# Diagonal attention scores as products on 32x32 tiles of the TensorE array, with another stored order

## The chip, the cores and the metric

The kernel runs on one core of a Trainium2 chip. A core has a matrix engine (TensorE, "PE" in the profile; its weight loads are listed apart as "PEld"), a vector engine (VectorE, "DVE"), a scalar engine (ScalarE, "ACT"), GpSimd ("POOL") and a queue that issues transfers (SyncE, "SP"). The metric is the device time in microseconds of one execution, as the median of several runs; lower is better.

## The reference

Two independent layers on 2048 tokens of width 640, joined side by side in the output. Layer A is a short causal filter of k, multiplied by v, then a long convolution over the whole sequence (by Fourier transforms), times q. Layer B is attention with 32 heads of 20 channels in four segments of 512 tokens: causal softmax within a segment, and a linear memory of the segments before. Only layer B is touched:

```python
qs, ks, vs = (q[:, :, s].copy(), k[:, :, s].copy(), v[:, :, s].copy())
logits = jnp.einsum('bhqd,bhkd->bhqk', qs, ks) * scale + mask
p = _softmax(logits, axis=-1)
a_dot = jnp.einsum('bhqk,bhkd->bhqd', p, vs)
...
num = jnp.einsum('bhld,bhde->bhle', pq, M)
den = jnp.einsum('bhld,bhd->bhl', pq, z)[..., None] + 1e-06
a_mem = num / den
o = g * a_mem + (1.0 - g) * a_dot
M = M + jnp.einsum('bhld,bhle->bhde', pk, vs)
```

Here `mask` is strongly negative where the key lies behind the query in time, so of the 512 x 512 scores of a segment and head only the lower triangle counts.

## The kernel before, in words

**Units.** Layer B is worked in eight units `u`: segment `u // 2`, half `u % 2` of the heads (16 heads, as four groups `gg` of four heads `hl`). Layer A is worked in five channel blocks `dp` and mixed in between. The transposed keys and queries of a unit lie in the tile `KQT`: the 32 partitions from `32 * hl` on belong to head `hl` of each group, 20 of them channels, one the bound that keeps the exponentials small, the rest mask rows.

**Fills.** The scores of a head group are made in "fills" of 512 columns and four heads: two groups of two PSUM banks, one bank a head. `fill` records the products on PE and then two exponentials on ACT, each over two banks, that write the tile `ET`. There are three kinds: "A" (`below`: blocks under the diagonal), "J" (`joined`: blocks of two head groups in one fill) and "D" (`diagonal`: the four 128 x 128 blocks on the diagonal). With five fills for two head groups a unit has ten, of them four of kind D: 32 D fills in the kernel. `weighted` then multiplies `ET` with the values `Va` and with the memory `Mbd`, in products of shape 128x128; DVE divides (`rr`, `o`, `o_s`).

**The diagonal fill.** `diagonal` records 32 products. First sixteen of keys with queries: for each of four key blocks `kc`, one for each head, 32 rows of the array (the head's partitions) and all 128 columns (the block's keys), 128 queries moving. Their 32 rows include the mask rows, which blank the coarse parts of a block's upper triangle. Then sixteen mask products on 32x32 tiles of the array: for each sub-block `i` of 32 keys and each head, `mleft` times `mright` (both in the constant `pack`) adds a large negative number to the fine triangle of all four blocks at once. All accumulate in the head's bank. In the profile the score products are `ps<-KQT 32*128 32x128` and the masks `ps<-pack 32*32 32x128`; the products of A and J fills are `ps<-KQT 21*128`.

**Order.** Nothing schedules at run time. `Recorder` collects 1446 operations (a whole fill's products are one operation, its two exponentials two more), and `issue` writes them out in the order of the table `ORDER`, with PSUM banks from the table `BASE`. Each engine works through its own instructions strictly in that order, and waits are set from the data. The string `EVICT` says for each of 235 evictions of PSUM whether ACT (0) or DVE (1) copies it. Almost all profile rows carry the line of `issue`, L259, so they are told apart by tile names.

Of the kernel before, what the change touches and what calls it, by code (L numbers as in the profile page):

```python
# [924 lines left out]
ORDER = r"""
c-jrs17i>h7zNOKKjd1rYuUE#mTlX%Z7$ccZQHhOoA3RJb5bBFaw8DQkP@j73#pL?X^|Z1kRBNj8}X44aRFpR9^^$NWI{m{LSaNiR768&WJOG5K{n(=6a*kL5+fcGAU_<5qzH;44iZar6hI6KlwwFN;U$8^lr)l6
nxHM3qa})?1WKY5N~1MWNI8^88H7SaDT{0pNwOmsk|4X}kY>m!L=f6QPzAXpx8#vT$cemC9W_uJiVCQRv{Du6#84A;P#3jO5A6^Gl~5Tu&=jpu4bdc)M3>l-M3PDiWR~{GBK6S_jgUYZBcY^}RFY3ZBaXzC4(N{F
=z%M;1Yyt_U65Z2NLVyLM--Ay=!stFgTCmBg3=G&kW2<3xeP=I;z@kzk3krWAsCJ*5>)~uvSgG@(q9Hh1*s@Kq>?N|ddVOoq_7N=a3~^6(Njjsa2X?|q>QY<N|csi7%Ssss*FH!DItq6PzK3RDJkP+f=rg8GDV8X
NGwBTS&ks-CB3DeOp{eujnP<)HCT(XQbo$kC>bpirJPKX=`spK0scfysVeKR9@S(Qs>^OPlEzX?#-O&;ks2}%d(cGc%3jQnda?l<F&5)7Q(8+K*@o@-DZgYB-b!29ft?7C37C#P@=p57X8gu1nJx9Dp-?Acumnp3
*@CT@BmXc&R86O#g|w8pGEYQX$tU?OpXHD2!&FShBpk$RIfOS7R=>zsX)4X7nJkn=au(+hMuRb5PT~}%;UX5uejGqJ4XtwkjiA499_{1;!s{jckWSKBx=2@PFCC<#tdkA0UQXi-E~A@tmxy{8e=!$VFb_v@469|0  # L930
1ZZTPftfgt6NsX-FdJ*-DwfJJc`qO2CYH-L`7ZlpzckewXr@s$n*ISPJRr_cTp=rEm4xPXgyCQLCyOOSmdHnmp$qU0%K6wR(bZU$5l~%g=vLV#*ARm-xm)(i9@#EO5R026HaE)_xs8|_OJnOnIV6YW7Iw%^*(I*u
aR;?|7x!@wp)?BHXdI2owt8Hu@ubw#`r1XKF)Z8Z35m`JsHsOJuEx`Fe1u3Ep2y?|PRVIGDi3i+&Ppwfz;kk5F33f>B#&`f+UpZ^)~D#I&GjW-poJ#Y<eE%tYX|M9b+myt)JED^BQg>bX-iG4tu%m<`5f^zfezJS
`V6n|8t?EParg<Jkwg<}Dow3vGy%J5T5Y1~^bJ~Tdd;A3kx>IRK2vBWO{pL75s4X(NmxXSYIjY}K*nVc&8)>V9aAwi(=#cPF^l%nteQ=;YYL`h4z12K?4-RlE%)nd&8cs+k7i&lt*aSXTnA_g?W_IthThbY`b3}V
Rr!kknu#@8Pzz~c9jJr!n%<OKa$WE0J<Y;|%*sT(Bbk|vHF#HYYhHb(&oz(M;%9xU@ASSt&>YOC`SrTokVb64!TJT+*^u>EpVy>-e$qOu%ON^kM`$T6t!1>V_SDDvQD5muZOkuPPRr|8y(jmjqE^yxT0uLoBfo29
9i?M5NUP{*En`2ms^(-T{?c38nYs8t%32fN*2y|mr)XshvYJ-QUPx}{VN<@8-#S*uX+^7K<25fUv#33j=W<7j*&qF@6LgYJ)Z4O_%?QiKYFgcDSaVL(={iGa>MUKXA-Y8W>1=Jm{0!nlc_feJiO|Ga@`tX_Rk~8w
u>ga0j?UG2I$sy)LT$y?tim>I%cZ(p3)?a+#P?dnN?AL8(Dq!X>$S9PW<f5}!Ysmvx<R{eqi)hix>>jARxQRC`tpAyR_hwwrbStn#aV*oxK>|@*?PLwvrx8OtJn_Rsa;v$x-+zewOzVf_h>h6Vh`@s;#R_{S{N&5
<*k8j<X{fraE@R}>(2p<XpyXu)wVhoU;{abLph8+S(2sL&>GuFj$$|qZyUIayIGzU*wi9eWQ%G$xRX(ApT@LU*34pC9P7<KjBC*>hHYVA_G5FaYw_%<w6N$_&3bVwTiP~mX9a6*X)K+svcq=7#<G=_W*Mfmw3gbM
SR0FPZEZAD*?CKE87+fduxobR#&HZ2*mx$iM3&f+SW>%am+XKhw-gp=$MuAsveTByGFuj#$QyQmH|>ZX)q`wjl~|Dzc+lEgSL<foZ50pMaht?@mdx(j2|H<r^spY{VV=}e+R3`uWZt)|md&zT4(n_=?V%;}T=vKU
J-MgwBRtC9*4O&jRl8+Vc#Ow6m5*&2^H^TXXZfvw-L@Xq({kHEEohm&mmSkIe$LW*7N5a8_Q0OlQ_JJe?V08Ee%9YQSVx=A1)R?Tmd?}rOdhpkc7i84$tK$rdtoo_l@+qAp3P_T6i;)Y4YFArY(s3Q&E-^^X1P4K
ujXZ&Zu2<I_HZxH*cCf#Gi;^}w|xxee$KKv9AP7El#REER>()&7#nL7EQCur&I<ZsF5wxzw)ghIF6(K%q95%7&vOk6`x(8cmvpuj@JxPIQ+rOIYx8WrEwF`lmccg1u5*#y;C<faWft`-{A71{mk;=mpRJgGvBh?d  # L940
S9y((c$2qS-0$(KUg8o9v8A@mmfH$@WAE&(t+ds4PD}WCU1KHv34hox%itOPF&A<Xf7)03Zr?1WFJme%?O{Bem+~@R)|WG^m-FBD$DZ-8J?BOKGdTSzBl-Vb_zDKNxqB!N?JIdfBYSw?ViA3-Met3w*`jzfkM1!%
rbqRce8E^A+v9j#kLTt66)SrckMBXA&ue&1ujQ|q-`{Ypt+#cy!8TfU&*5)b!7KVZ7V!jL$rE}aPwZ8_x+n2!{(;+Vhb8r)Ufb(<UEgEFe5Y-*_x#Bp+-o1X&vscWZ|$GB-#)XR@3#8hz#DoaZ{v-<gLm|=?Bq?n
sefTJZ|*Jp8@qW+@8RA3J5@|vLdkF+;lKEsf7#aC`vD6rfB27KB%Fkm&fd;P`Y4A`M0$EJ@9llOt9SAKKG_HOKp*6Ny`K;EAwJs2_&lHPGkl7V^>IGmXM3>E@tHo?r}{LX<x70AFYxg`!6*78U+5ve$o~UpIlx>
"""
# [76 lines left out]
```

## Time and profile before

| | us |
|---|---|
| median of three runs (270.0 to 271.64) | 270.61 |
| the profiled execution, its own time | 267.98 |
| its span, first to last instruction | 266.2 |
| busy: PE / DVE / ACT | 257.2 / 245.0 / 242.8 |
| PE, score products of D fills (512) | 13.7 |
| PE, mask products of D fills (512) | 8.8 |
| ACT, exponentials (160) | 158.5 |

How to read it: each engine's busy time is the time in which at least one of its instructions was under way. A product on PE is shown from its start until its result has landed, so products overlap one another; the distance between starts says how fast they follow, not their length. A group row gives line, engine, operation, output and inputs, the shape on the array as rows*columns, the moving data, the count, the busy time and the mean length in nanoseconds. In a table of stretches the columns are the stretch and its length, the busy time of each engine with its instructions, the granted clock of TensorE as a share of full speed, the share of the DMA engines and GB/s.

### The profile page before, as it was taken

The page shows a single profiled execution, that of the slowest core. Times are in us where ns is not written, and L with a number is a line of the kernel's source. Part 1 is how long each engine was busy: PE and PEld are TensorE (multiplying, and loading weights), DVE is VectorE, ACT ScalarE, POOL GpSimd, SP SyncE. Part 2 cuts the span into 40 slices and gives each one's busy share as a digit, 9 for nine tenths or more (in the row PEclk, how much of TensorE's full clock was granted, in tenths as well). Part 3 has the DMA queues.
Part 4 walks back from the last instruction along what each step waited for, and adds up shares of the span by engine and source line. Part 5 has one row for each costly group of instructions (what it writes and reads, how often), then busy time and mean ns, then how long its engine had stood idle before and what let it go on. Part 6 is the DMA issues. An engine that isn't in the chain of part 4 may idle for free.

```text
span 266.2 us, 10257 instructions
## 1 busy us (share of the span) xinstructions
PE 257.2 (97%) x4471; PEld 192.8 (72%) x4471; DVE 245.0 (92%) x406; ACT 242.8 (91%) x361; POOL 2.6 (1%) x9
## 2 busy tenths in 40 slices
PE   8999999999999999999999999999999999799994
PEld 3787777768777868768777778777777777556882
DVE  2679799999999999999999999999999999989951
ACT  2478999999999999999999999999999999989943
POOL 3000000000000000000000000000000000000000
PEclk9999999999999999999999999999999999989999
DMA  6999699969979799998999999776937379226142
GB/s 176 245 286 204 153 214 196 250 180 158 164 160 234 153 226 142 161 231 199 110 248 189 220 192 194 101 164 143 170 89 184 81 133 137 55 64 147 38 98 99
DMA packets 127945, 43.86 MB, mean 165 GB/s; under 512 B 118455, under 2 KB 125516, under 8 KB 127772
## 3 DMA queue, kind: packets, MB, share of 16 engines
q1 hardware_dynamic: 127772, 43.14, 82.1%
q8 instruction: 35, 0.57, 0.9%
q0 software_dynamic: 128, 0.07, 0.2%
q14 instruction: 10, 0.08, 0.1%
...
## 4 chain that ended last, share of the span: by engine, by line
PE 82%; DVE 10%; ACT 4%; issue 3%; DVEq 0%; ACTq 0%
PE ps L259 82%; ACT ET L259 3%; DVE F L259 2%; DVE pq L259 2%; DVE Kh L259 1%; DVE Xh L259 1%; DVE o_s L259 1%; DVE o L259 1%; DVE vt L259 0%; DVE KQ L259 0%; DVE rr L259 0%; DVE qabs L259 0%; DVE Y L259 0%; ACT outb L259 0%; DVE outb L259 0%
## 5 line engine op out<-in xcount | busy, mean ns | idle before, releaser
L259 ACT ACTIVATE ET<-ps 128x1024 bf16<-128x1024 f32 x160 | 158.5, 1057 | 3.3 <-PE ps L259 2.7
L259 PE MATMUL ps<-wqkv,xT 128*128 128x320 bf16 x480 | 77.2, 301 | 0.3 <-ACT ET L259 0.3
L259 PEld LDWEIGHTS <-xT 128*128 128x128 bf16 x640 | 58.3, 98 | 26.0 <-issue 4.7
L259 PE MATMUL ps<-Va,ET 128*128 128x21 bf16 x1280 | 41.0, 172 | 0.0
L259 PEld LDWEIGHTS <-ET 128*128 128x128 bf16 x1280 | 38.7, 96 | 2.1 <-issue 1.2
L259 PE MATMUL ps<-KQT 32*128 32x128 bf16 (+3 forms) x896 | 33.4, 242 | 1.0 <-ACT ET L259 0.7
L259 PEld LDWEIGHTS <-Wf 128*128 128x128 bf16 x320 | 29.7, 98 | 6.4 <-issue 1.7
L259 PE MATMUL ps<-wo,xT 128*128 128x320 bf16 (+4 forms) x160 | 25.7, 304 | 0.4 <-ACT ET L259 0.4
L259 ACT CAST KQ<-ps 128x320 bf16<-128x320 f32 x54 | 24.2, 487 | 1.5 <-PE ps L259 1.3
L259 PEld LDWEIGHTS <-KQT 32*128 32x128 bf16 (+1 forms) x896 | 14.1, 92 | 15.5 <-issue 13.6
L259 PE MATMUL ps<-vt,Wf 128*128 128x256 bf16 x160 | 22.9, 273 | 0.0
L259 PE MATMUL ps<-kT,Wf 128*128 128x256 bf16 x160 | 21.1, 273 | 0.2 <-DVE pq L259 0.2
L259 ACT ACTIVATE F<-ps 128x512 bf16<-128x512 f32 x33 | 20.0, 633 | 1.3 <-PE ps L259 0.8
L259 ACT CAST F<-ps 128x512 bf16<-128x512 f32 x34 | 20.0, 635 | 0.8 <-PE ps L259 0.4
L259 PE MATMUL ps<-Y,Wi 128*128 128x256 bf16 x160 | 20.3, 273 | 0.1
L259 PE MATMUL ps<-Mbd,PqT 128*128 128x84 bf16 x96 | 18.0, 202 | 1.1 <-ACT ET L259 0.9
L259 DVE TENSOR_TENSOR Y<-Y,pq 128x2048 bf16<-128x2048 bf16 (+1 forms) x20 | 18.7, 946 | 0.0
L259 DVE TENSOR_TENSOR pq<-Xh,Kh 128x2048 bf16<-128x2048 bf16 x15 | 18.3, 1217 | 0.0
L259 PEld LDWEIGHTS <-Wi 128*128 128x128 bf16 x160 | 15.1, 98 | 2.6 <-issue 0.4
L259 ACT ACTIVATE PP<-KQ 128x1280 bf16<-128x1280 bf16 x12 | 15.8, 1314 | 1.2 <-DVE KQ L259 1.2
L259 PEld LDWEIGHTS <-kr 128*128 128x128 bf16 x116 | 14.4, 148 | 1.9 <-issue 0.6
L259 DVE TENSOR_TENSOR pq<-ps,pq 128x512 bf16<-128x512 f32 x20 | 13.6, 683 | 0.2 <-PE ps L259 0.2
...
## 6 DMA issues: line engine op xcount, KB each, us to landing
...
```

The source lines that it names most:

```text
L259: f(*[fix(a) for a in args], **{k: fix(v) for k, v in kw.items()})
```

## The change

`diagonal` no longer uses `block` with 32 rows. Each score product of 32 rows and 128 columns is split by keys into four on 32x32 tiles of the array: sub-block `i` of 32 keys goes to the columns and PSUM partitions from `32 * i` on. Four rounds (one a key block) of sixteen products follow each other, then the sixteen masks as before: 80 products in a fill instead of 32, all on 32x32 tiles. The values in PSUM are the same. `block` loses its argument `rows`. The tables `EVICT`, `ORDER` and `BASE` are replaced.

```diff
-        def block(bank, hl, g, kc, q0, n, rows=DH + 1, **kw):
-            r = slice(32 * hl, 32 * hl + rows)
+        def block(bank, hl, g, kc, q0, n, **kw):
+            r = slice(32 * hl, 32 * hl + DH + 1)
             nc.tensor.matmul(bank, lhsT=KT[r, g, 128 * kc:128 * kc + 128], rhs=QT[r, g, q0:q0 + n], skip_group_check=True, **kw)
...
         def diagonal(gg):
             def parts(heads):
                 for kc in range(4):
-                    for hl, bank, r, g in heads:
-                        block(bank[:, 128 * kc:128 * kc + 128], hl, gg, kc, 128 * kc, 128, rows=32, start=(kc == 0), stop=False, grp=g)
+                    for i in range(4):
+                        for hl, bank, r, g in heads:
+                            nc.tensor.matmul(bank[32 * i:32 * i + 32, 128 * kc:128 * kc + 128], lhsT=KT[r, gg, 128 * kc + 32 * i:128 * kc + 32 * i + 32],
+                                             rhs=QT[r, gg, 128 * kc:128 * kc + 128], start=(kc == 0), stop=False, grp=g, skip_group_check=True)
                 for i in range(4):
                     for hl, bank, r, g in heads:
...
-EVICT = ("0001000000001001000010010000000001000100000000000100000000000000000010100010010001001000010010000100001001000000000000100"
+EVICT = ("0001110000101000001000010000000100100000000000000000010000000000000001100011000000000110010000000010000010000000000000"
...
 ORDER = r"""
-c-jrs17i>h7zNOKKjd1rYuUE#mTlX%Z7$ccZQHhOoA3RJb5bBFaw8DQkP@j73#pL?X^|Z1kRBNj8}X44aRFpR9^^$NWI{m{LSaNiR768&WJOG5K{n(=6a*kL5+fcGAU_<5qzH;44iZar6hI6KlwwFN;U$8^lr)l6
+c-jq?gO(To3<NjHrnYU{wyi7fYU^s-wr$(CZQHiZf0#EjDG&pZ5djgA65){#u@DcjkqD`f7^#s4X^{><eiT4VBu6r&M*<W?ArwXiWJX40LJ`D=qbQ0Y3$h{`k{}17AS!YrI<g}v5^5sNgS<$saS>f(XdEQh6dG0=
...
```

Three places show what that does to the streams.

The first is PE at the first D fill of the program (unit 0, head group 0), where each product has its weight load ahead of it; `KQT0_96` is the tile `KQT` of the first half, and the last two numbers of a row are the output's partitions and columns. Before:

```order
L259 MATMUL ps_61<-wqkv_79,xT0_105 128x320
L259 LDWEIGHTS KQT0_96 [waits DMAHW5_49]
L259 MATMUL ps_61<-KQT0_96 128x128 [waits Activation_49]
L259 LDWEIGHTS KQT0_96
L259 MATMUL ps_61<-KQT0_96 128x128
...
L259 LDWEIGHTS pack_85 [waits DMASW2_49]
L259 MATMUL ps_61<-pack_85 32x4x32
```

And now:

```order
L259 MATMUL ps_61<-wqkv_79,xT0_105 128x320
L259 LDWEIGHTS KQT0_96 [waits DMAHW6_49]
L259 MATMUL ps_61<-KQT0_96 32x128 [waits Activation_49]
L259 LDWEIGHTS KQT0_96
L259 MATMUL ps_61<-KQT0_96 32x128
...
L259 LDWEIGHTS pack_85 [waits DMASW0_49]
L259 MATMUL ps_61<-pack_85 32x4x32
```

Between the first score product and the first mask there were 16 pairs of load and product that write 128 partitions; now there are 64 that write 32. The masks write 32 partitions in both, so the shape no longer changes inside the fill. The first product's wait, for ACT to have emptied its banks, stays at the head of the fill.

The second is ACT in the stage in which the last units' scores are worked (tiles `ET_...` are exponentials, `Va` and `bT` evictions). Before:

```order
L259 ACTIVATE ET_123<-ps 128x1024 [waits PE_49]
L259 ACTIVATE ET_123<-ps 128x1024 [waits DVE_49]
L259 ACTIVATE ET_120<-ps 128x1024 [waits PE_49]
L259 CAST Va_95<-ps 128x16x20 [waits DVE_49,PE_49]
L259 ACTIVATE ET_120<-ps 128x1024
L259 ACTIVATE ET_119<-ps 128x1024 [waits PE_49]
L259 ACTIVATE ET_119<-ps 128x1024
L259 ACTIVATE ET_121<-ps 128x1024 [waits PE_49]
L259 CAST bT_117<-ps 128x128 [waits DMAHW1_49,PE_49]
L259 ACTIVATE ET_121<-ps 128x1024 [waits DVE_49]
```

And now:

```order
L259 ACTIVATE ET_123<-ps 128x1024 [waits DVE_49,PE_49]
L259 ACTIVATE ET_123<-ps 128x1024 [waits PE_49]
L259 ACTIVATE ET_120<-ps 128x1024 [waits PE_49]
L259 ACTIVATE ET_120<-ps 128x1024 [waits DVE_49]
L259 ACTIVATE ET_119<-ps 128x1024 [waits PE_49] x2
L259 ACTIVATE ET_121<-ps 128x1024 [waits PE_49]
L259 ACTIVATE ET_121<-ps 128x1024 [waits DVE_49,PE_49]
```

The fills follow in the same order; one eviction of values has moved to a later place on ACT, and that of the bounds (`bT`) to DVE.

The third is DVE at the end of the program (`pq` is layer A's output, `xT` the transposed attention output of the last segment, `PP` its projection). Before:

```order
L259 TENSOR_TENSOR pq0_87<-ps_61,pq0_87 128x4x128 x3
L259 CAST xT1_106<-ps_61 128x512
L259 TENSOR_TENSOR pq0_87<-ps_61,pq0_87 128x4x128
L259 RECIPROCAL rr0_126<-ps_61 128x32
L259 TENSOR_TENSOR o_s0_118<-ps_61,rr0_126 128x8x80
L259 RECIPROCAL rr1_127<-ps_61 128x32
L259 TENSOR_TENSOR o_s0_118<-ps_61,rr1_127 128x8x80
L259 CAST PP_89<-ps_61 128x512 x2
```

And now:

```order
L259 TENSOR_TENSOR pq0_87<-ps_61,pq0_87 128x4x128 x4
L259 RECIPROCAL rr0_126<-ps_61 128x32
L259 TENSOR_TENSOR o_s0_118<-ps_61,rr0_126 128x8x80
L259 RECIPROCAL rr1_127<-ps_61 128x32
L259 TENSOR_TENSOR o_s0_118<-ps_61,rr1_127 128x8x80
L259 CAST xT1_106<-ps_61 128x512
L259 CAST PP_89<-ps_61 128x512 x2
```

The one eviction of `xT` has moved behind the last divisions: DVE takes another of the five pieces than before, and ACT the one that was DVE's.

More of the change, by code (lines that the diff above doesn't have):

```diff
@@ L919 @@
 TAP2 = (2, 3, 4)
-EVICT = ("0001000000001001000010010000000001000100000000000100000000000000000010100010010001000010010000100001001000000000000100"
-         "000000000010100100000100000000000000001101001010100000000001001000110001101010101110100101000000100000000100010001001")
+EVICT = ("0001110000101000001000010000000100100000000000000000010000000000000001100011000000000110010000000010000010000000000000"
+         "001100000001001101000000000000010000001101001000000000100101010001000100110101001000100000000110100000110010000110100")
 KQW, FW, WW = 1, 1, 1
@@ L925 @@
 ORDER = r"""
-c-jrs17i>h7zNOKKjd1rYuUE#mTlX%Z7$ccZQHhOoA3RJb5bBFaw8DQkP@j73#pL?X^|Z1kRBNj8}X44aRFpR9^^$NWI{m{LSaNiR768&WJOG5K{n(=6a*kL5+fcGAU_<5qzH;44iZar6hI6KlwwFN;U$8^lr)l6
-nxHM3qa})?1WKY5N~1MWNI8^88H7SaDT{0pNwOmsk|4X}kY>m!L=f6QPzAXpx8#vT$cemC9W_uJiVCQRv{Du6#84A;P#3jO5A6^Gl~5Tu&=jpu4bdc)M3>l-M3PDiWR~{GBK6S_jgUYZBcY^}RFY3ZBaXzC4(N{F
-=z%M;1Yyt_U65Z2NLVyLM--Ay=!stFgTCmBg3=G&kW2<3xeP=I;z@kzk3krWAsCJ*5>)~uvSgG@(q9Hh1*s@Kq>?N|ddVOoq_7N=a3~^6(Njjsa2X?|q>QY<N|csi7%Ssss*FH!DItq6PzK3RDJkP+f=rg8GDV8X
@@ L929 @@
[L929 to L940, printed above, removed]
@@ L941 @@
-S9y((c$2qS-0$(KUg8o9v8A@mmfH$@WAE&(t+ds4PD}WCU1KHv34hox%itOPF&A<Xf7)03Zr?1WFJme%?O{Bem+~@R)|WG^m-FBD$DZ-8J?BOKGdTSzBl-Vb_zDKNxqB!N?JIdfBYSw?ViA3-Met3w*`jzfkM1!%
-rbqRce8E^A+v9j#kLTt66)SrckMBXA&ue&1ujQ|q-`{Ypt+#cy!8TfU&*5)b!7KVZ7V!jL$rE}aPwZ8_x+n2!{(;+Vhb8r)Ufb(<UEgEFe5Y-*_x#Bp+-o1X&vscWZ|$GB-#)XR@3#8hz#DoaZ{v-<gLm|=?Bq?n
-sefTJZ|*Jp8@qW+@8RA3J5@|vLdkF+;lKEsf7#aC`vD6rfB27KB%Fkm&fd;P`Y4A`M0$EJ@9llOt9SAKKG_HOKp*6Ny`K;EAwJs2_&lHPGkl7V^>IGmXM3>E@tHo?r}{LX<x70AFYxg`!6*78U+5ve$o~UpIlx>
+c-jq?gO(To3<NjHrnYU{wyi7fYU^s-wr$(CZQHiZf0#EjDG&pZ5djgA65){#u@DcjkqD`f7^#s4X^{><eiT4VBu6r&M*<W?ArwXiWJX40LJ`D=qbQ0Y3$h{`k{}17AS!YrI<g}v5^5sNgS<$saS>f(XdEQh6dG0=
@@ new lines @@
+AsSjCjfT@~npK;kI7*=eN<)!d%OMiVqdCf;I%=RKYC=!}RZtc=G^f@=F67dj$gO!a00~hM1|krR5rk%_jTWebs;GuaXo(OAuMsq{CefH$8Fdj^^J){M)z*lm!DxsENU7;Gs&+s$&8%6pBf6j~>Z2Y)q7B-j2jXi_
+q|#34jBe<K-bkSB&>e9#pXS#B+8%un8r?OD_Rx453SG4?7NMJF)QFl%BWZsO)*+fylj&tGq)X68`(XeEqJmb^ike<C=wKAo#VD*pupBE8Tl;DpEv2hbTGwDG%IHcI*OFR9SD}P1#WD=TaLh+P?XM#+2t#$4R@N#S
+2BUPe_ST{rpvAPTmeVmhNyln=9f@(;K*wuCZKR{I6T47Vt7)JHX-%!JHMEx2);c;-Cu>U$*4@~H&kC8MZ*&1#=~k@8Hmt)S{i0KKBR1i!{=hV?tJ_gu>*;VEp(Aw%He)@;V1jPJES;{S5EdISKnH41?WM2uwa(C)
+I$P)HIE=+!jK@SY(@AKq6L1jw&_WO37e4BKeA0#Zp+EJPPQh;#Qwwd4wTU)Wvon~hwD}s!PN2QE);4+p7jY6laTYVtK_{cF&O$pqj8h0}rxC_F>Lpyp0u5)K^c>FPgLc*~8s7e5p03sPIu+BfPLJRyBHC=s!B>3O
@@ new lines @@
+Rk~Uu*)bePWSfo|SffjHnO?(EeW&mBH~t`sMKzZYvRC)%SN*0}A+lc&L8Y<5n%Hu^f)%<_O(-E{p)S@x`d1g}7Tv1bw7S)>P;vv;5nW<PNQ-XK>=t(E9^I`m>>Fa*c8w{qWP@(hd6<h$x>;{xhknNaJ*aLW?2y*6
+x^^3Z7Gyg$w1kmkdR&`YGmBs+G_pjIIM&+QSXc=scW@7f^{C#(eZ;kgh$_(}mL1Wm5)Ren0fMcS)wB9`QcvkwJ+0v-f}GRy+QA;-3C`#Ry{MNowk5G-med;9D>Srf5>eXPW3;nKQqyW#LhERWthu$Y#1_w<;|1bd
+Cwq!#7-WO(EfQE9NoA?+CEg*nw6sRH&#vf4d_thS#v8<wG}gtETMA2QX)T?lw+xm{GFm2kj}Pc<MXadBmqe0W(n%^wFU72@C6+9f)v{T3OCfP3rDTwdl3K3mb<JU!t-Ga>w30-UN_)#`J*>Euv{zQb5=c$yX}#>V
+C6pj}Y)|Zt-L>9U&<a^?>uY^1i+o05>u3G#jb)O|a@}s&UCk!<w42qC0hZhH*j2k`Uy#?X>TSKF_w2r9l^pWXZs<VEWpC}K){(lB&+^+Rt0hmZfYp=Q^1+7KFdJ&m?2CQ22J*<(NPTH2rL44-v9k8n%2|0EZrNp|
@@ new lines @@
+wUu^K!A4jkX)G13l2x`U7RUgrYVD<ie6tBQ(SkV1nn+W*Y1Qn$-m)K7ojK*F73C<a!P{1hqiu|pVOi#qihO79?U&_|-}cffF}IAh@wQI>{1@j_9cRz9GOKW*J=eTaS^nB&n_^QfzpRzT_ClxGbemy|?3O;zhuTb<
+%W}&nEC1uIoMp3Zg|(0ZGRMB#OsgU#WUd)oO0cw&dA7us*?fDXk9Da9NNZ^$g`^Y<N>M2+#bmvZ5A2~8kp;Ha*4sKO%;NIgUf2fPXq#-at&}2MW!1Prw%ArH%{5km&Jf%r8)dbXm5>ZzXog}(DJONg-FDbc+htv4
+w^d~wmScH_X9RAunykf$EGc`eI9IX+UuqZGYeS?YYqON}kua>sq0(78$p9HB-K4x!kiODS!f}`klI}8C8Za#T%W#Rrow7@!Fa~2X7GpCq>$8XSlsJsb&9X)ITU174LpI`8*(TB1OL|LVZkHXBhUs{KY1xDaIYLTH
+8EML^tSHy`L{l;qM@vgyU?sW8W^B%QY{4;di0PS{!ED9W%)pF1V23$UMoD}oU_vHhVkY4^o@X+q;5a$SQ#@wLdECazb>84zX5w+4uoKM8gLcTWaKDU~19H;tunjvgDerNDbmn0@V#nBp$vuTX;6cgCY|PF>(w;e(
@@ new lines @@
+leyTDN&T=qWCyO2BhrJ(yeIQ8FDFSaPLzDi&jNhJ+&n7B<R))%vUFv4cH<Eq<yq$O+sx}%n8u&6Ak%tpKIRm8!l}}SnLUg5Wm`UFJC5fBPLo2M$gG~tr^|6UA@|vj{W*XGIf#=uh0pndlQ~09$|<?T!Mx1VJj30x
+M^;NZPw%s32&Zy7XUR;N#$0~N_DXKwCv#*dhjBPZa3s&lTq)?II8VlK9LMq{7s^pvEQ{o{6!KSm#|w7J-t)9Ak<q+pA2@?K{j!~tD^}Rg%Nd)^Ih@ORoX-VZ$eEnQGjdOE$$hykm*ld1<YyN33-XEA<bhn5D{@ut
+$XzMsi@2CexRlGdoGW-k9?EOpl*e+`&e<Dg@|0fO-|{<u@{y$S`LaO1@CU!LgfEqn{*9qLw1@H3UcgIxDPJZ}rHq&LU;NEK{L5z&!6Q0+6<1UIe=MBt9?8RcIA0-8B!pj-kiL=OeG?;lRFC4DxrJ-^LZW#LkM8CC
+yshPOc`h+MmdExuUfwHv6))m(J;3964G;8u{!(5^kZ1QCp20JEeqYD+tl*XWjl7n(Qqkjk0#E3PJh3P7s$Siz`8#<pySbHnSkr5JE#J$1{2)Vo19xyIhx#_Q@Rq)vA0^o9cwMjO^}T_&_4eM#ze{6p;!XXBwDV8W
@@ L944 @@
+&_7FO{~}#{kPr4|-rT>*Px<<P6sWt{)kCQ3e*Tg_@>_=aaBt<UJ*0-x&>BYn%Kt>GY8&t1oqURS^lskWdw5Up<ukmu_wl~o&-?oTAK?>xj1TltKH5k6SfA+=eX39L$v(}e`#7KF<9)U-^aZ}i=lEQo=ktBB{{!DY
+z+3
 """
 BASE = r"""
-c-mD`2@=F049aEv|Bp8U+S%!NGzyXsGc&iEIp!<d_$ynp?uoV~;xUmuBPV{wIX$-uIGde;#lW}cYv2uQ&dSI^??E`w2KEGp<Cg19m!1N5LZ3t5#`)nmqj9sKi1-9+K}AAA;T~1CvPmG%Ta7mwBcREECR@A=68nR0
-+&K6a`<+Ae;GBy3UyWG7qi7)qhXz)iDi~q*p;$>(Nm0WM)`G0p$Bo=l2<BHW+xm+&ILX$~=TdicE%3HHUC)*4OT)vI?obz%YR$iXwKVy3JLvXG=&UvB?a7;RC!~16{f3UME@EE<=B0XWFnxIvUwZF5yE++N>TQ2+
@@ L948 @@
-wyMe(`{^Q%u7+xTc|(<JC~|dH+7B1i1#$
+c-mD`36caM2t&^Q|9By!9k;9610ji#5SJs`e@aR8%0zlTJ!(g?_uk{=Oho(4aqhi0?5gL<n~eERM+%6B3PpVZcQ_0P%OgN4;tNh3*bdYn!=MS63>p+?f~bRU^gDh7moht%71Y1Hj$MK$p<&m8dk>FZu61F3aPWTB
+KZJ=md=li&sH{Hl$&h2L3*xVub=aw3GZi>~)hSgg84Pz-VC?OJtAdt&Ke-tB=u@gYa3`V8_!a^c>v|&3>E&Xc>v>-E^)|>DSP2-Cud2Ljupf+L(Z9tq-de79<^Q_8ks|UzEZ9ZG7uM^?B7AjDMM*dPS$!TIcAm2H
+6zFl^N&j_^Kl7(qh-U23MH!|)$U6n9
 """
```

## The prediction

> **What bounds the kernel now.** First the page: its span, its engines, and the chain of waits by engine.
>
> ```profile
> span 266.2 us, 10257 instructions
> PE 257.2 (97%) x4471; PEld 192.8 (72%) x4471; DVE 245.0 (92%) x406; ACT 242.8 (91%) x361; POOL 2.6 (1%) x9
> ...
> PE 82%; DVE 10%; ACT 4%; issue 3%; DVEq 0%; ACTq 0%
> ```
>
> PE is on the chain for 82% of the span, but DVE and ACT are busy for over 90% too. A mean over stages says little, so next comes the table of busy time by stretch (us busy of each engine, then the granted clock).
>
> ```profile
> 0.00:27.00 27.00, 25.06 (x213) 18.59 (x214) 18.78 (x49) 15.97 (x31) 2.65 (x9) 1.00 0.98 230
> 27.00:215.00 188.00, 187.71 (x3360) 141.87 (x3359) 185.21 (x297) 185.78 (x279) 0.00 (x0) 1.00 0.92 175
> 215.00:246.00 31.00, 28.35 (x599) 19.72 (x596) 29.53 (x43) 29.83 (x39) 0.00 (x0) 0.94 0.51 99
> 246.00:263.00 17.00, 16.12 (x308) 12.60 (x307) 11.50 (x20) 11.16 (x15) 0.00 (x0) 1.00 0.24 64
> ```
>
> In the long middle stretch PE idles for 188.00 - 187.71 = 0.3 us, ACT for 2.2 and DVE for 2.8: all three are full, and PE is only the fullest. From 215 to 246 us PE idles 2.65 us, and the other two less. The chain in order of time says the same:
>
> ```profile
> 26.36 55.11 PE ps L259 x887
> ...
> 81.48 19.91 PE ps L259 x366
> ...
> 107.52 34.75 PE ps L259 x596
> ...
> 142.28 72.33 PE ps L259 x1345
> ...
> 229.34 2.90 ACT ET L259 x3
> ...
> 246.34 16.14 PE ps L259 x306
> ```
>
> PE sets the pace from 26 to 214 us and from 246 to 262 us; between them the chain jumps among DVE, ACT and PE, as in the row of the exponentials (ACT ET) at 229.34.
>
> **The change part by part: the fills.** The edit touches 32 diagonal fills (eight units, four head groups). This is one of them in the timeline of PE and of its weight loads (start, length, shape, count):
>
> ```profile
> 39.81 0.39 PE L259 MATMUL ps<-skd,kr 128*128 128x256 bf16 x3
> 40.14 0.40 PE L259 MATMUL ps<-KQT 32*128 32x128 bf16 x16
> 40.47 0.28 PE L259 MATMUL ps<-pack 32*32 32x128 bf16 x16
> 40.68 0.31 PE L259 MATMUL ps<-wqkv,xT 128*128 128x320 bf16 x1
> ...
> 40.14 0.23 PEld L259 LDWEIGHTS <-KQT 32*128 32x128 bf16 x16
> 40.47 0.14 PEld L259 LDWEIGHTS <-pack 32*32 32x32 bf16 x16
> ```
>
> ```profile
> L259 PE MATMUL ps<-KQT 32*128 32x128 bf16 x512 | 13.7, 217 | 1.0 <-ACT ET L259 0.7
> ...
> L259 PE MATMUL ps<-pack 32*32 32x128 bf16 x512 | 8.8, 226 | 0.0
> ```
>
> The sixteen score products (each 217 ns by the group row) run as four rounds of four. Their last one starts 0.40 - 0.217 = 0.18 us after the first, so a round takes 0.18 / 3 = 0.06 us. The masks do not start 0.06 us after the last round but at 40.47, which is 0.47 - 0.32 = 0.15 us after it: changing the shape from 32x128 to 32x32 costs 0.15 - 0.06 = 0.09 us. The sixteen masks start within 0.28 - 0.226 = 0.054 us, 3.6 ns apart. The next product of full shape starts 0.16 us after the last mask. The fill, from its first product to the next work, takes 40.68 - 40.14 = 0.54 us.
>
> After the change there are 64 score pairs (a weight load and a product each), in four rounds of sixteen. A round is bounded by the stream, 0.06 us, and by sixteen pairs at 3.6 ns, 0.058 us; I take 0.06. Four rounds make 0.24 us, then the masks follow in the same shape: 0.054 us to the last one, 0.16 us to the next work, 0.45 to 0.46 us in all. That saves 0.085 us a fill, 32 x 0.085 = 2.7 us. Upper bound: pairs at 3.6 ns without any step, 80 x 0.0036 + 0.16 = 0.45 us, saves 0.09. Lower bound: weights are not ready when a round starts. A small load's record lasts 0.14 - 15 x 0.0036 = 0.09 us, which would make rounds of 0.15 us and a fill of 0.81 us, 0.27 us longer than now. The nearest row on this is a product that is tiled by columns and loads new weights on each tile for four rounds:
>
> ```profile
> 195.91 0.40 PE L259 MATMUL ps<-qabs,A 128*16 128x128 bf16 x16
> ...
> L259 PE MATMUL ps<-qabs,A 128*16 128x128 bf16 x112 | 2.8, 220 | 0.2 <-DVE A L259 0.2
> ```
>
> Its rounds are (0.40 - 0.22) / 3 = 0.06 us apart, so loading lay beneath the stream there, and I take the loads as hidden.
>
> The Trainium skill speaks against this: "TensorEngine Tiling (Array Packing)", section "Gotcha 2: Feature Incompatibilities", says that column tiling excludes the fast weight load, and "TensorE: Matmul & The Clock Gate", section "LDWEIGHTS (loading the stationary operand)", prices a load at its columns over 1.2, an estimate of 27 ns for 32 columns. Four such loads in the open would make 0.11 us and eat the saving; the trace's 0.06 us rounds on column tiles do not show one in the open, though with 16 columns only.
>
> **The other edits.** Counted in the two stored orders, the changes of shape outside the fills go from 170 to 173: 3 x 0.09 = +0.3 us on PE. Evictions change engine: DVE gets two more and ACT two fewer (51 instead of 49 of 235). The two rows of a typical one cost nearly the same:
>
> ```profile
> L259 ACT CAST KQ<-ps 128x320 bf16<-128x320 f32 x54 | 24.2, 487 | 1.5 <-PE ps L259 1.3
> ...
> L259 DVE CAST KQ<-ps 128x320 bf16<-128x320 f32 x10 | 4.9, 497 | 1.3 <-PE ps L259 1.3
> ```
>
> So DVE gains 1.0 us and ACT loses 1.0 us of work over the run; from zero to all of that falls into the middle stretch, and I take half. It lies beneath PE as long as DVE has idle time there. The stored order moves operations by a few places, in the end stage too, where the last evictions swap engines one for one; I count that at zero, with 0.5 us to either side for its transfers (SP issues the same 157, some earlier and some later). The added instructions must be fetched:
>
> ```profile
> q8 instruction: 35, 0.57, 0.9%
> ```
>
> PE's rows in the stored program go from 8944 to 12016, a third more; by this row that is a third of 0.9% of the DMA engines' span, which I put at zero.
>
> **What reaches the end.** The fills by stretch, with the masks' group (sixteen a fill):
>
> ```profile
> 27.00:215.00 188.00, 6.90 (x400) 3.45 (x400) 5.22 (x15) 0.00 (x0) 1.00 0.92 175
> 215.00:246.00 31.00, 1.38 (x80) 0.69 (x80) 0.19 (x1) 0.00 (x0) 0.94 0.51 99
> 246.00:263.00 17.00, 0.55 (x32) 0.28 (x32) 0.00 (x0) 0.00 (x0) 1.00 0.24 64
> ```
>
> 25 fills lie in the middle stretch, 5 between 215 and 246, 2 behind. The five are counted at nothing: ACT and DVE set the pace there. The middle's 25 x 0.085 = 2.1 us is just under ACT's idle 2.2 and DVE's 2.8 less 0.5 us; what hides ACT and DVE is used up by this, and any more would not show. With the last two, 27 x 0.085 = 2.3 us, less 0.3: **2.0 us shorter**. The profiled execution took 267.98 us (1.8 us around its span), so 266.0. The median of the three runs is 270.61, 2.6 above it; the same difference gives **268.6 us**.
>
> **Rivals.** *The cover is gone at once.* ACT and DVE are 98.8% and 98.5% busy in the middle; if their small waits are not waits for PE but the grain of two strict queues, they stay, and only a part of the 2.1 us shows. Against it: the chain has PE alone for 182 of those 188 us. This gives 0 to 1.3 us, about 270.0.
>
> *The pairs are not supplied fast enough*: the side of slower. Now a fill is 32 pairs, 64 instructions; after it is 80 pairs, and no row shows more than 32 at the fast pace. The slowest pace that the profile has for small products, each with a load of its own, is this:
>
> ```profile
> 46.24 0.42 PE L259 MATMUL ps<-Va,ET 128*128 128x21 bf16 x11
> ...
> L259 PE MATMUL ps<-Va,ET 128*128 128x21 bf16 x1280 | 41.0, 172 | 0.0
> ```
>
> That is (0.42 - 0.172) / 10 = 25 ns a pair. If 32 pairs stand ready when a fill starts, and the other 48 come at 25 ns each from then on, the last mask starts at 48 x 0.025 = 1.2 us, the fill takes 1.36 us in place of 0.54, and the kernel 32 x 0.82 = 26 us more: 297 us. It decides from the pace at which 48 pairs no longer fit before today's last mask, 0.54 - 0.16 = 0.38 us: 8 ns a pair. Below that nothing is lost. Weights in the open, the lower bound above, would cost 32 x 0.27 = 8.6 us, 279 us, and belong to this case. For it: nothing in the trace is as long. Against it: after a wait in the middle of a fill (the product at 231.37 below) the fourteen left-over products still take the usual 0.40 us, and the masks follow at their usual distance:
>
> ```profile
> 231.37 0.40 PE L259 MATMUL ps<-KQT 32*128 32x128 bf16 x14 [0.36 <-ACT ET L259]
> ...
> 231.70 0.28 PE L259 MATMUL ps<-pack 32*32 32x128 bf16 x16
> ```
>
> The Trainium skill has a rule on this side: "TensorE: Matmul & The Clock Gate", section "Wait — 56ns, not 53.3ns?", says that products never start less than about 25 ns apart, however small; by it 64 score pairs would be 1.6 us a fill, an estimate that comes to the price just worked out. The masks' 3.6 ns contradict it for a burst on different tiles; for a longer run no row decides, since that page's opening table gives TensorE a queue of 64 entries, which is just one fill of now.
>
> *The stage from 215 to 246 us turns worse or better.* Its granted clock is 0.94, so 0.06 x 31 = 1.9 us of full clock were lost in it; PE idles there for ACT. A shorter fill leaves PE idler, and another order can move, add or remove that dip, or add waits: up to 2 us more (271 to 272), or, where the dip goes, up to 2 us less on top of the forecast (about 266.5).
>
> **How the numbers follow.** Forecast (267.3 to 269.2): 0.49. Cover gone (269.2 to 270.6): 0.22. Supply too slow (272 and far above): 0.13. The stage worse: 0.08, half of it beyond the bound. The stage better: 0.08. A measurement of this kernel can tell about 0.5%, 1.35 us, from no change. Faster by more: 0.49 + 0.08, 0.57. Within: the 0.22 and half of the stage worse, 0.26. Slower: 0.13 and the other half, 0.17. The range goes from 266.0 to 272.0 us: it leaves out the supply case with its 0.13 and a few hundredths at either end of the last rival, and takes in the upper bound of the saving (32 x 0.09, 0.2 us more than counted). The likeliest case alone is 267.3 to 269.2.
>
> **What would show it right or wrong.** In the changed kernel's timeline a fill should be one group of 64 products and one of 16 masks, 0.24 us apart, with the next work 0.45 us after the first product; the pairs 3.6 ns apart within a round. Masks that start at 0.3 us or later after the first product mean rounds longer than 0.06 us; gaps from the 33rd pair on mean supply. PE's busy time should fall by 2 to 3 us with DVE's and ACT's unchanged, and the idle time of ACT and DVE between 27 and 215 us should nearly vanish; if PE instead shows waits for ACT or DVE there, the cover was gone. The forecast is wrong if a fill takes 0.5 us or more, or if the fills are short and the middle stretch is as long as before.

## The result, and the profile after

The changed kernel takes **281.87 us** (median of 4 runs, 280.01 to 283.09) against 270.31 us (4 runs) for the kernel before on the same chip: a ratio of **1.043**, 95% interval 1.034 to 1.053. Slower, by far more than can be put down to the measurement, and outside the predicted range of 266.0 to 272.0.

The page of the changed kernel, its span, its engines, its instruction fetches and its chain of waits:

```profile
span 280.1 us, 13339 instructions
PE 267.4 (95%) x6007; PEld 203.0 (72%) x6007; DVE 249.8 (89%) x408; ACT 243.3 (87%) x359; POOL 2.5 (1%) x9
...
q8 instruction: 47, 0.77, 1.2%
...
PE 83%; ACT 6%; DVE 5%; issue 3%; DMA 1%; SPq 0%; ACTq 0%
```

PE was to lose 2 to 3 us of busy time and gained 10.2; DVE and ACT are as before to 5 us. The middle stretch in the table by stretch (us busy of each engine, count, then the granted clock), and the group row of the exponentials with its idle time behind the bar:

```profile
27.00:215.00 188.00, 184.73 (x4226) 139.99 (x4225) 176.56 (x276) 175.11 (x263) 0.00 (x0) 0.99 0.92 170
...
L259 ACT ACTIVATE ET<-ps 128x1024 bf16<-128x1024 f32 x160 | 158.5, 1048 | 14.4 <-PE ps L259 13.9
```

DVE and ACT, 98% busy there before, idle for 11 and 13 us: they wait for PE's scores. The cover was not the question; PE itself got slower. The timeline shows where (start, length, shape, count):

```profile
39.65 0.84 PE L259 MATMUL ps<-wqkv,xT 128*128 128x320 bf16 x5
40.43 0.73 PE L259 MATMUL ps<-KQT 32*32 32x128 bf16 x64
40.95 0.35 PE L259 MATMUL ps<-pack 32*32 32x128 bf16 x16
41.22 0.58 PE L259 MATMUL ps<-wqkv,xT 128*128 128x320 bf16 x3
```

From the first product to the next work: 41.22 - 40.43 = 0.79 us (798 ns in the trace) in place of 0.54. The last score starts about 0.73 - 0.22 = 0.51 us after the first, where the forecast's four rounds put it at some 0.23; the masks take 0.35 us in place of 0.28. The same fill once more, counted: stretches that all start with it and end later and later, the score products and loads alone (busy and count of PE, of PEld):

```profile
40.44:40.48 0.04, 0.04 (x16) 0.04 (x17) 0.00 (x0) 0.00 (x0) 1.00 1.24 282
40.44:40.56 0.12, 0.12 (x32) 0.12 (x33) 0.00 (x0) 0.00 (x0) 1.00 1.22 277
40.44:40.67 0.23, 0.23 (x32) 0.20 (x33) 0.00 (x0) 0.00 (x0) 1.00 1.25 285
40.44:40.69 0.25, 0.25 (x34) 0.21 (x34) 0.00 (x0) 0.00 (x0) 1.00 1.26 286
40.44:40.75 0.31, 0.31 (x41) 0.27 (x42) 0.00 (x0) 0.00 (x0) 1.00 1.26 287
40.44:40.81 0.37, 0.37 (x48) 0.33 (x49) 0.00 (x0) 0.00 (x0) 1.00 1.26 286
```

Three regimes: 32 products by 0.12 us, as forecast; **none for the next 0.11 us**; then 7 in each 0.06 us. In the trace the later ones, masks too, start 8.3 ns apart in an unbroken row, from 0.25 us to the last mask at 0.64.

A second loss stands in the list of waits and in the chain in order of time. Before, PE's products waited nowhere for "issue" (time in which the engine waited for nothing that the profile shows). Now:

```profile
PE ps L259 <- issue: 3.6, 6, 1.2
```

```profile
48.93 1.17 issue
...
159.63 0.37 issue
...
176.22 0.62 issue
...
244.58 1.08 issue
```

The first of them is in the middle of a fill (timeline):

```profile
48.37 0.56 PE L259 MATMUL ps<-KQT 32*32 32x128 bf16 x43
50.10 0.30 PE L259 MATMUL ps<-KQT 32*32 32x128 bf16 x21 [1.17 <-issue]
```

and the granted clock is at half for some 3 us behind it:

```profile
50.50:51.50 1.00, 1.00 (x10) 0.72 (x6) 0.74 (x3) 0.80 (x1) 0.00 (x0) 0.50 0.85 287
51.50:53.60 2.10, 2.10 (x10) 1.18 (x9) 0.66 (x2) 1.63 (x3) 0.00 (x0) 0.50 0.95 375
```

**The account.** 32 fills x 0.258 us = 8.3; stalls of PE at issue, 3.6; 3.1 us at half clock, 1.5. That is 13.4 of the 280.1 - 266.2 = 13.9 us between the two spans. The clock's term is gross: the kernel before had a dip of its own (0.94 from 215 to 246 us), which is gone here. By the mean clocks of the two profiles, 0.994 and 0.992, the net term is an estimated 0.6 us; the sum is then 12.5, and 1.4 us stay open.

### The profile page after: what moved, and what is told of

The parts are those of the page before. It is cut to its first block, busy times and chain, and to the rows that moved or that the text cites. A ratio compares the mean times of both kernels' runs of the same rounds, so it can differ in the third digit from the quotient of the medians.

```text
span 280.1 us, 13339 instructions
## 1 busy us (share of the span) xinstructions
PE 267.4 (95%) x6007; PEld 203.0 (72%) x6007; DVE 249.8 (89%) x408; ACT 243.3 (87%) x359; POOL 2.5 (1%) x9
## 4 chain that ended last, share of the span: by engine, by line
PE 83%; ACT 6%; DVE 5%; issue 3%; DMA 1%; SPq 0%; ACTq 0%
PE ps L259 83%; ACT ET L259 5%; DMA Y<-in_B_x_dram 1%; DVE pq L259 1%; DVE Xh L259 1%; DVE F L259 1%; DVE Y L259 0%; DVE o_s L259 0%; DVE outb L259 0%; DVE o L259 0%; ACT outb L259 0%; SPq L259 0%; DVE PP L259 0%; DVE rr L259 0%; DVE vt L259 0%
## 5 line engine op out<-in xcount | busy, mean ns | idle before, releaser
L259 ACT ACTIVATE ET<-ps 128x1024 bf16<-128x1024 f32 x160 | 158.5, 1048 | 14.4 <-PE ps L259 13.9
L259 PE MATMUL ps<-KQT 32*32 32x128 bf16 (+3 forms) x2432 | 44.8, 229 | 2.0 <-issue 1.4
L259 PEld LDWEIGHTS <-KQT 32*32 32x32 bf16 (+1 forms) x2432 | 24.7, 88 | 18.7 <-issue 15.9
L259 PEld LDWEIGHTS <-Wf 128*128 128x128 bf16 x320 | 29.2, 98 | 6.3 <-issue 1.6
L259 ACT CAST KQ<-ps 128x320 bf16<-128x320 f32 x52 | 22.6, 462 | 3.9 <-PE ps L259 3.6
L259 PE MATMUL ps<-kT,Wf 128*128 128x256 bf16 x160 | 21.7, 273 | 0.0
L259 ACT CAST F<-ps 128x512 bf16<-128x512 f32 x33 | 19.1, 629 | 0.1
L259 PE MATMUL ps<-Mbd,PqT 128*128 128x84 bf16 x96 | 17.9, 202 | 0.8 <-ACT ET L259 0.6
```

What stands on the lines that cost most here:

```text
L259: f(*[fix(a) for a in args], **{k: fix(v) for k, v in kw.items()})
```

## The experiments

Three theories. *Theory 1*: TensorE's instructions are not supplied fast enough; about 32 pairs (a weight load and a product each) stand ready when a fill starts. *Theory 2*: the new stored order costs the time. *Theory 3*: repeated rounds on the same 32x32 tiles are slow in themselves, by their loads or their banks.

**old_order and new_order: the two parts of the change apart.** The first is the changed kernel with the three old tables:

```diff
-EVICT = ("0001110000101000001000010000000100100000000000000000010000000000000001100011000000000110010000000010000010000000000000"
...
+EVICT = ("0001000000001001000010010000000001000100000000000100000000000000000010100010010001000010010000100001001000000000000100"
...
```

> The new diagonal under the stored order, evictions and banks of before. Theory 1 (the instructions of a fill's small products come too slowly: about 66 stand ready, a new one reaches the head some 254 ns after the first was taken, then one comes each 4.17 ns): a typical fill's last mask again 0.62 to 0.66 us after its first product, next work at 0.78 to 0.82 us, and the kernel 280 to 284 us. Theory 2 (the new stored order costs the time): 270 us, and fills as in before. Theory 3 (a third and fourth round on the same 32x32 tiles is slow in itself): as theory 1.

The second is the other half, the old loop of 16 score products under the new tables:

```diff
-                    for i in range(4):
-                        for hl, bank, r, g in heads:
...
+                    for hl, bank, r, g in heads:
+                        block(bank[:, 128 * kc:128 * kc + 128], hl, gg, kc, 128 * kc, 128, rows=32, start=(kc == 0), stop=False, grp=g)
```

> The diagonal of before under the new stored order, evictions and banks. Theories 1 and 3: fills of 0.54 us as in before, no stall of 0.4 us or more behind an instruction fetch, and 269 to 272 us. Theory 2: 280 us and more.

Measured: old_order 285.03 us, ratio 1.062 (1.055 to 1.069), its ordinary fills 798 ns; new_order 267.39 us, ratio **1.0001** (0.997 to 1.004). The first is just above what was expected, the second below it (the kernel before took 267.55 us on this chip). Theory 2 falls: the tables by themselves cost nothing. The diagonal alone costs 6%, more than both parts together; the old order has 5.5 us of stalls at issue in place of 3.6, one of them 3.2 us, and a mean clock of 0.976.

**pause: the same products, with a rest after the 32nd pair.**

```diff
                 for kc in range(4):
+                    if kc == 2:
+                        for n in range(2):
+                            nc.tensor.matmul(heads[0][1], lhsT=self.ident[64:128, :], rhs=self.Drow[64:128, None, :].to_broadcast([64, 4, 128]),
+                                             start=False, stop=False, grp=heads[0][3], skip_group_check=True)
```

> The changed kernel with two products of 512 columns that add zero, put into each diagonal fill after its first 32 score pairs; the result is the same. Theory 1: TensorE is busy with the two for about 0.43 us, in which instructions come in again, so that pairs 33 to 64 take about 3.5 ns each, as the first 32 did, and only the masks behind them come at 4 to 8 ns. Theory 3: pairs 33 to 64 take 8.3 ns each with the pause too, 0.27 us for the 32. By either the kernel gets longer: 284 to 292 us.

Measured: 296.77 us (one run). The timeline of a fill, and the count from 41.32 us on, the first products after the rest (here of all shapes; the first number in a pair of brackets is PE's count):

```profile
40.51 0.33 PE L259 MATMUL ps<-KQT 32*32 32x128 bf16 x32
40.78 0.60 PE L259 MATMUL ps<-Drow,ident 64*128 64x512 bf16 x2
41.31 0.33 PE L259 MATMUL ps<-KQT 32*32 32x128 bf16 x32
41.56 0.35 PE L259 MATMUL ps<-pack 32*32 32x128 bf16 x16
```

```profile
41.32:41.44 0.12, 0.12 (x33) 0.12 (x33) 0.12 (x1) 0.00 (x0) 0.00 (x0) 1.00 0.11 24
41.32:41.55 0.23, 0.23 (x33) 0.19 (x33) 0.23 (x1) 0.00 (x0) 0.00 (x0) 1.00 0.09 20
41.32:41.62 0.30, 0.30 (x40) 0.24 (x40) 0.30 (x1) 0.00 (x0) 0.00 (x0) 1.00 0.09 20
```

Both groups of 32 take 0.33 us in all. Pairs 33 to 64, the third and fourth rounds on the same tiles and banks, are as fast after the rest as the first 32 (3.3 ns apart within a round in the trace, which the rounded columns of the prediction's row gave as 3.6), and the pause and the slow pace have moved behind them, to the masks. Theory 3 falls. The total was expected too low: with the two products and their changes of shape, 0.68 us lie between the starts of the 32nd and the 33rd pair, not 0.43, and the fill takes 1.33 us.

**queries32: as many pairs, of another shape.** Full 32x128 tiles, 32 queries each:

```diff
-  ... bank[32 * i:32 * i + 32, 128 * kc:128 * kc + 128], lhsT=KT[r, gg, 128 * kc + 32 * i:128 * kc + 32 * i + 32], rhs=QT[r, gg, 128 * kc:128 * kc + 128], ...
+  ... bank[:, 128 * kc + 32 * i:128 * kc + 32 * i + 32], lhsT=KT[r, gg, 128 * kc:128 * kc + 128], rhs=QT[r, gg, 128 * kc + 32 * i:128 * kc + 32 * i + 32], ...
```

> The changed kernel with its 64 score pairs cut another way: the full 32x128 tiles of before, 32 queries each, in place of 32x32 tiles with 128 queries; 80 pairs a fill as in the change, the same result. Theory 1 (a fill takes 32 pairs at once; the next come 0.2 us after the 17th was taken and then at 8.3 ns each): 33rd pair 0.25 us after the first, 64th at about 0.51, masks to 0.65 to 0.70, next work at 0.80 to 0.86 us, kernel 281 to 287 us. Theory 3 (a third round on a 32x32 tile is slow): there is no such round before the masks, scores are done at 0.22 to 0.24 us, next work at 0.52 to 0.54, kernel 267 to 268 us.

```profile
40.61 0.65 PE L259 MATMUL ps<-KQT 32*128 32x32 bf16 x64
41.19 0.28 PE L259 MATMUL ps<-pack 32*32 32x128 bf16 x16
```

282.25 us (one run), the next work 794 ns after the first product: as in the changed kernel, without a single score on a 32x32 tile. In the trace the first 32 pairs come in sets of four, 25 ns a set; from the 33rd, at 0.21 us, they are 8.3 ns apart. The pause before the 33rd that was expected is not there (more on this under pairs48). The masks sit behind a change of shape of 0.11 us again, and the last starts at 0.635 us, in the changed kernel, which has no such change, at 0.643: in a fill of 80 pairs that change of shape is free; by theory 1, because instructions come in during it.

**pairs48, pairs64, pairs32: the dose.** Fewer, longer rounds, which leave out the right scores of some blocks; the diff is of pairs48, and the rounds are (0, 256), (2, 128), (3, 128) in pairs64 and (0, 512) in pairs32:

```diff
-                for kc in range(4):
+                for kc, n in ((0, 256), (2, 256)):
...
-  ... 128 * kc:128 * kc + 128 ...
+  ... 128 * kc:128 * kc + n ...
```

> Two rounds of 16 products with 256 queries each in place of four with 128, so a fill is 32 + 16 = 48 pairs (96 instructions); the second half of each round's queries gets scores with the wrong keys, so the right scores of two of four blocks are left out. Theory 1: 254 + (96 - 66) x 4.17 = 379 ns to the last mask, the next work at about 0.53 us, as in before (0.54), and the kernel 268 to 272 us. If every pair beyond the 32nd cost 25 ns, the last mask would be at about 0.52 us and the kernel at 274. Theory 2: 280 us.

> Three rounds, the first with 256 queries, the others with 128: 48 + 16 = 64 pairs a fill. One block in four gets its scores with the wrong keys, the right ones are left out. Theory 1: the 17th pair starts at 0.11 us, the 33rd at 0.31, and the 31 after it take 8.3 ns each: last mask at 0.56, next work at 0.72 us, 0.18 us a fill more than before, 5.8 us, and one to four stalls of 0.4 to 1.8 us behind an instruction fetch: 274 to 279 us.

> One round of 16 products with 512 queries each in place of four with 128: 16 + 16 = 32 pairs a fill, as many as before. The right scores of three of four blocks are left out. Theory 1: all of it stands ready, the products start within 0.05 us, the masks follow when the streams end, at about 0.22 us, the last at 0.27, next work at 0.42 to 0.43 us: 0.115 us a fill less than before. The kernel is then 264 us (32 x 0.115 = 3.7 us) if nothing is late next, and 266 to 267.5 if ACT and DVE, 98% busy in the middle of before, hold it.

pairs48: 271.25 us (one run). The last mask came at 431 ns and the next work at 585, 0.05 us later than expected. The second round starts later here (its predecessor streams 256 queries), and the pause ends later with it: the 17th pair at 120 ns and the 33rd at 306, against 66 and 252 in the changed kernel. The later expectations took from this that the pause ends 0.19 us after the 17th pair. queries32 does not fit that (17th at 114 ns, 33rd at 214). What fits all three is how many queries a burst's first products have: with 32, 128 and 256 the 33rd pair starts 214, 252 and 306 ns after the first, 0.4 ns more for each query, so an estimated 0.20 us after the first product has streamed them. In queries32 the 32 pairs themselves take that long, hence no gap. That a place in the queue is filled again only when its product is through would explain it; no run tests that. pairs64: 279.08 us (one run), next work at 718 ns as expected, and three stalls, 4.4 us. pairs32: 265.43 us, ratio **0.992** (0.988 to 0.996). Its fill and its middle stretch:

```profile
39.78 0.43 PE L259 MATMUL ps<-KQT 32*32 32x512 bf16 x16
40.01 0.26 PE L259 MATMUL ps<-pack 32*32 32x128 bf16 x16
40.21 0.31 PE L259 MATMUL ps<-wqkv,xT 128*128 128x320 bf16 x1
```

```profile
27.00:215.00 188.00, 186.69 (x3384) 137.95 (x3384) 186.78 (x299) 185.79 (x281) 0.00 (x0) 1.00 0.91 176
```

With 32 pairs all on one tile shape a fill is 0.43 us, and of the 3.7 us that this takes from the fills 2.4 show in the medians (267.87 before), so the total lies between the two that were expected. DVE is then as full as PE.

**tiles64: scores on 32x64 tiles**, 48 pairs with the right result.

```diff
-                    for i in range(4):
+                    for i in range(2):
...
-  ... bank[32 * i:32 * i + 32, ...], lhsT=KT[r, gg, 128 * kc + 32 * i:128 * kc + 32 * i + 32], ...
+  ... bank[64 * i:64 * i + 64, ...], lhsT=KT[r, gg, 128 * kc + 64 * i:128 * kc + 64 * i + 64], ...
```

> Scores on 32x64 tiles, four rounds of 8, and the 16 masks: 48 pairs a fill, the same result. Theory 1: the 17th pair starts at 0.11 us, the 33rd not before 0.11 + 0.2 = 0.31, the 16 masks from there at 8.3 ns each, to 0.43, next work at 0.585 us: 0.045 us a fill more than before, 1.4 us, and a stall or two at an instruction fetch: 268.5 to 272 us. Without a limit of supply the masks would end at 0.36 to 0.38 us and the kernel be as before, 267.5.

```profile
40.09 0.43 PE L259 MATMUL ps<-KQT 32*64 32x128 bf16 x32
40.45 0.28 PE L259 MATMUL ps<-pack 32*32 32x128 bf16 x16
40.66 0.31 PE L259 MATMUL ps<-wqkv,xT 128*128 128x320 bf16 x1
```

272.23 us, ratio 1.016 (1.009 to 1.023). The total is just above the upper end of what was expected, and the fill is not as expected: the masks come at the fast pace (0.28 us for the group), since the 33rd pair stands behind a change of shape of 0.14 us, in which by theory 1 the instructions came in. The fill is 0.57 us. The profile of this kernel is only 2.8 us longer than that of before; the rest of the median's 4.4 us is not explained by it.

**zeros80: the kernel before with 48 products more.** The old 32x128 scores, then 48 products of the masks' shape with zero weights, then the masks.

```diff
+                for n in range(3):
+                    for i in range(4):
+                        for hl, bank, r, g in heads:
+                            z = 32 * ((hl + 1) % 4)
+                            nc.tensor.matmul(bank[32 * i:32 * i + 32, :]..., lhsT=self.ident[r, z:z + 32], rhs=self.mright[r, None, :]..., ...)
```

> The kernel before with 48 products of the masks' shape that add zero, between its scores and its masks: 80 pairs a fill, as in the change, the same result. Theory 1: the 17th pair starts at 0.33 us, the 33rd at 0.38, then nothing until 0.33 + 0.2 = 0.53, then 47 pairs at 8.3 ns, to 0.92, next work at 1.08 us in place of 0.54: 32 x 0.54 = 17 us more, 284 us, and 0 to 7 us of stalls at instruction fetches. If pairs cost 3.6 ns however many there are: 48 x 0.0036 = 0.17 us a fill, 273 us.

```profile
40.33 0.40 PE L259 MATMUL ps<-KQT 32*128 32x128 bf16 x16
40.66 0.60 PE L259 MATMUL ps<-pack,ident 32*32 32x128 bf16 x48
41.05 0.35 PE L259 MATMUL ps<-pack 32*32 32x128 bf16 x16
41.33 0.31 PE L259 MATMUL ps<-wqkv,xT 128*128 128x320 bf16 x1
```

288.58 us (one run), 20.7 more than before, where 3.6 ns a pair would have made 5. The fill is 1.00 us, not 1.08, because the burst begins anew behind the slow rounds of four and the change of shape. Counted from the first zero product, zero products and masks alone:

```profile
40.66:40.79 0.13, 0.12 (x32) 0.00 (x0) 0.00 (x0) 0.00 (x0) 1.00 1.28 289
40.66:40.90 0.24, 0.23 (x32) 0.00 (x0) 0.00 (x0) 0.00 (x0) 1.00 1.26 281
40.66:41.00 0.34, 0.34 (x42) 0.00 (x0) 0.00 (x0) 0.00 (x0) 1.00 1.22 270
```

Again 32 pairs, a pause to 252 ns after the first of them in the trace, then 8.3 ns. The 32 belong to what stands ready when a dense run begins, not to the fill. The changed kernel shows the same where a fill is interrupted: where PE waits for banks ahead of the third pair (fill at 260.65 us) the pause stands before the 35th, and behind the long stall ahead of the 44th (fill at 48.37 us) before the 76th.

**shifted: where the long stalls sit.** The changed kernel with 64 products more in the first microseconds:

```diff
                 with rec.one():
+                    for m in range(64 if n == 0 else 0):
+                        nc.tensor.matmul(g.ap[:, 0, 0:16], lhsT=idle[:, 0:128], rhs=idle[:, 128:144], start=True, stop=True, grp=g)
                     nc.tensor.matmul(g.ap[:, 0, 0:WARMC], lhsT=idle[:, 0:128], ...
```

> The changed kernel with 64 small products (128 instructions) more among the first ones, while TensorE waits for its first transfers; the result is the same. It moves the whole later program by half of a 256-instruction block. Theory 1, second part (a stall comes where a block of 256 instructions is used up before the next block, 16 KB, has come): the stalls of 0.4 to 1.4 us, at 50.1, 138.0, 160.0, 176.8 and 245.7 us in the changed kernel, go from those places of the program to others; each still ends 1.3 to 1.8 us behind the end of an instruction fetch. Rival (these stalls are waits for data at these places, or belong to these fills): they stay at the same places of the program. Kernel 278 to 286 us by either; the ordinary fills keep their 0.80 us.

286.11 us (one run), just above what was expected; ordinary fills 798 ns. The chain in order of time, and one place in the timeline that had no stall in the changed kernel:

```profile
48.70 2.34 issue
...
80.92 0.78 issue
...
110.64 0.79 issue
...
208.54 0.88 issue
...
213.06 0.37 issue
```

```profile
80.22 0.71 PE L259 MATMUL ps<-KQT 32*32 32x128 bf16 x61
81.70 0.23 PE L259 MATMUL ps<-KQT 32*32 32x128 bf16 x3 [0.78 <-issue]
```

The stalls left their places in the program. They did not leave their places in the row of instructions: counted along PE's loads and products in the order of the trace, those of the changed kernel end at 1469, 5302, 6326, 7091, 8625 and 10672, those of this one at 1469, 2747, 4026, 6580, 8625, 8881 and 10672. Divided by 256 all of them leave 176 to 189, and so do those of pairs64 (185, 181, 176). A fetch is 0.77 MB / 47 = 16 KB, which for 12016 rows in 0.77 MB is 256 instructions. Each stall of the two kernels ends 1.3 to 1.8 us after the last fetch's record ended (one 2.3 us). So they stand at the border of two blocks and wait for the next block; no data or fill at those places holds PE. What starts a fetch was not tried.

**All together.** For each kernel, from its one profiled execution: the fill; what 32 of them add to 32 x 0.540 us; PE's stalls at issue from the list of waits; the clock, as (0.994 - its mean) x span, 0.994 being that of before and the product an estimate; their sum; and how much longer the span is than 266.2 us.

| kernel | pairs | fill, us | fills | stalls | clock | sum | span longer by |
|---|---|---|---|---|---|---|---|
| changed | 80 | 0.80 | 8.3 | 3.6 | 0.6 | 12.5 | 13.9 |
| old_order | 80 | 0.80 | 8.3 | 5.5 | 5.1 | 18.9 | 17.9 |
| shifted | 80 | 0.80 | 8.3 | 5.9 | 1.7 | 15.9 | 18.1 |
| queries32 | 80 | 0.79 | 8.1 | 3.0 | 3.6 | 14.7 | 14.3 |
| pairs64 | 64 | 0.72 | 5.7 | 4.4 | 0.3 | 10.4 | 11.0 |
| pairs48 | 48 | 0.585 | 1.4 | 1.7 | 0 | 3.1 | 3.3 |
| tiles64 | 48 | 0.57 | 0.9 | 1.7 | 0 | 2.6 | 2.8 |
| pairs32 | 32 | 0.42 | -3.7 | 0.2 | 1.9 | -1.6 | -0.5 |
| zeros80 | 80 | 1.00 | 14.7 | 3.0 | 3.7 | 21.4 | 20.6 |
| pause | 80 + 2 | 1.33 | 25.3 | 3.6 | 0.3 | 29.2 | 28.8 |
| new_order | 32 | 0.54 | 0 | 0.2 | 0 | 0.2 | 1.5 |

In shifted the added products themselves put off all that follows by 1.2 us (the fill at 40.43 us starts at 41.66), which is more than half of its rest. The other rows close within 1.4 us, from 32 pairs to 80 and over three shapes. No version here that computes the reference beats the kernel before; new_order equals it.

## Why the prediction was wrong

**The step that failed** is the working of the new fill: "A round is bounded by the stream, 0.06 us, and by sixteen pairs at 3.6 ns ... Four rounds make 0.24 us". It holds for two rounds. The pace of 3.6 ns was read from sixteen masks and used for eighty pairs. Measured, the fill has 32 pairs at about that pace, 0.13 us of pause and 47 pairs at 8.3 ns: 0.12 + 0.13 + 0.39 = 0.64 us to the last mask, then the 0.155 us to the next work. That is 0.258 us more than before a fill, where 0.085 less was forecast. pause, queries32 and zeros80 show it to be a matter of the number of pairs in a dense run, not of tile shape, rounds or banks. Every product in these kernels has a load of its own, so no run tells whether the limit counts pairs or single instructions, and the queue itself stands in no trace: that supply is what runs out is the reading that fits all runs.

**The rival had the mechanism, with the size wrong.** "The pairs are not supplied fast enough" put the border at 32 pairs and got a chance of 0.13. Its price, 25 ns a pair, came from full-size products and was three times too high: hence 297 us and not 282. Its break-even of 8 ns a pair was met almost exactly by the real pace, and by that alone the case would have been judged harmless; it left out the pause, which decides. Its evidence against, the fill cut short at 231.37 us, had 14 + 16 pairs to go, fewer than 32, and could not speak to it. The Trainium skill, "TensorE: Matmul & The Clock Gate", gives TensorE in its opening table a queue of 64 entries; the trace agrees, with 32 to 33 pairs of two instructions in the first burst, and this row should have weighed more than the row of masks. No run shows the 25 ns between starts of its section "Wait — 56ns, not 53.3ns?" as a floor on products of different tiles: these came 3.3 and 8.3 ns apart; the sets of four in queries32, which use the same four tiles again, were 25 ns apart.

**A near hit that was luck.** The prediction's lower bound, weights not ready when a round starts, gave a fill of 0.81 us and 279 us, close to the measured 0.80 and 281.87. Its mechanism is refuted: it needed rounds of 0.15 us, and in the trace the second round starts 0.07 us after the first, in pause the fourth 0.07 us after the third.

**The fetches put at zero** were the second error. Their share of the DMA time was small and stayed small (0.9% to 1.2%); it was the wrong measure. What counts is how soon 256 instructions are used up against how long the next 16 KB take to come. That cost 3.6 us of stalls. Behind one of them came 3.1 us at half clock, 1.5 us; that the stall brought it about is not shown.

**What held.** Loads of 32 columns do lie beneath the stream: the first 32 pairs, and pairs 33 to 64 after a rest, start within 0.12 us. The change of shape inside the fill does vanish (the first mask follows the last score by 8 ns in the trace), but queries32 shows it to be worth nothing once supply sets the end. The stored order and the evictions at about zero: new_order, 1.0001. The cover: in pairs32 the fill was 0.115 us shorter and two thirds of it showed, so that ACT and DVE would have let a saving of the forecast's size through in good part; the sign came from PE alone. The dip of the clock between 215 and 246 us went (1.00 in place of 0.94), the better side of that rival, but another of the same size came at 50 us.
